# Two leading weight pieces of a fused attention and SwiGLU kernel: each load cut into two transfers over unequal numbers of partitions

## Chip, cores and metric

The kernel runs on one core of a Trainium2 chip. The metric is the device time of one execution in microseconds (us). The core has five engines that run side by side, each in its own program order: TensorE (PE in the profile, its weight loads as PEld), VectorE (DVE), ScalarE (ACT), GpSimd (POOL) and SyncE (SP), which here issues nearly all the transfers. Transfers are carried out by 16 DMA engines. An engine waits for another, or for a transfer, through semaphores.

## The reference

Lightning attention with a decay for each head feeds a SwiGLU layer. Cut to what is computed (4 batches, 8 heads, 768 positions, 64 wide; 3072 tokens, model width 512, hidden width 1536):

```python
for b in range(nb):                                  # blocks of 64 positions
    intra = np.einsum('bhic,bhjc->bhij', qb, kb) * Dmask[None]
    intra = np.einsum('bhij,bhjd->bhid', intra, vb)
    inter = np.einsum('bhid,bhde->bhie', qb * lam_pow[None], kv_state)
    out[:, :, sl] = intra + inter
    kv_state = lam_block[None, :, None, None] * kv_state + \
        np.einsum('bhsd,bhse->bhde', kb * rev_pow[None], vb)
x = out.transpose(0, 2, 1, 3).reshape(3072, 512)
g = x @ w_gate                                       # 512 x 1536
y = (g / (1 + np.exp(-g)) * (x @ w_val)) @ w_out     # 1536 x 512
```

All inputs and the output are float32. The weights that matter here are `w_gate` and `w_val`.

## The kernel before

**Tiling.** Attention is done in 12 groups of 256 positions of one batch. Each pair of groups makes one token tile of 512 tokens, and the SwiGLU layer runs over six such tiles. A weight matrix of 512 x 1536 lies in SBUF as 128 partitions by 4 row chunks by 1536 columns in bfloat16 (`wg_sb`, `wv_sb`). The hidden width is walked in 12 columns blocks of 128, called `fc` below.

**Order.** The schedule is written out by hand: every engine executes its instructions in the order in which the code emits them. The stretch that the change touches is the start. SP (and for two transfers ACT) loads k, q and v of groups 0 and 1 in halves (line 100, `load_fp32`), and then the weights. The weights come as float32 pieces through `w_piece` (line 218 issues): a piece covers some columns of `w_gate` and the same columns of `w_val`, all 512 rows, as one transfer each. The first two pieces are one `fc` block wide (128 columns, 256 KB for each matrix); all later ones are two blocks wide (512 KB for each matrix). The raw float32 tiles come from a pool of ten buffers that k and q of later groups share; a narrow piece holds gate and value in one buffer.

After landing, a piece is cast to bfloat16. The first narrow piece is cast by GpSimd in lines 652 and 653, the second by GpSimd through `w_cast` (line 226), the gate part of a wide piece by ScalarE and its value part by GpSimd (line 226; the first value part in two halves at line 672). TensorE then uses it: line 519 is the gate product (`ffn_gate`), line 534 the value product (`ffn_val`). Block 0 is computed for half the tokens before group 1's attention is finished, and from block 2 on the blocks run over 512 tokens, with later transfers (`w_piece`, `load_group`) and casts attached to them as a plan. The load of group 2 (k, q) stands on SP after the weight pieces of blocks 6 to 9; its q is cast by GpSimd (line 278, `cast_half`) and transposed by TensorE (line 294, `pe_transpose`) after block 8. The output product is line 552.

In the raw load each partition receives 4 runs (one for each row chunk) of 128 columns, 512 bytes each, so one partition's share of a narrow transfer is 2 KB. All the loads in question stand in one queue:

```python
    w_piece(0, 1)
    w_piece(1, 2)
    w_piece(2, 4)
    w_piece(4, 6)
```

Of the kernel before, what the change touches and what calls it, by code (L numbers as in the profile page):

```python
# [19 lines left out]
@with_exitstack  # L20
def kernel(
    ctx: ExitStack,
    tc: tile.TileContext,
    q: bass.AP,
    k: bass.AP,
    v: bass.AP,
    lam: bass.AP,
    moe_w_gate: bass.AP,
    moe_w_val: bass.AP,
    moe_w_out: bass.AP,  # L30
    out: bass.AP,
):
    nc = tc.nc
    with tc.manual_schedule():
        _body(ctx, tc, nc, q, k, v, lam, moe_w_gate, moe_w_val, moe_w_out, out)


def _body(ctx, tc, nc, q, k, v, lam, moe_w_gate, moe_w_val, moe_w_out, out):
# [169 lines left out]
    wv_d = moe_w_val.rearrange("(c p) f -> p c f", p=128)  # L208
    wo_d = moe_w_out.rearrange("(c p) m -> p c m", p=128)

    def w_piece(c0, c1, eng=None):
        cs = slice(c0 * 128, c1 * 128)
        n = (c1 - c0) * 128
        if n == 128:
            both = raw_pool.tile([128, 2, MC, n], FP32, name="wraw", tag="raw")
        for j, (w_sb, w_d) in enumerate(((wg_sb, wg_d), (wv_sb, wv_d))):
            t = both[:, j] if n == 128 else raw_pool.tile([128, MC, n], FP32, name="wraw", tag="raw")
            (eng or nc.sync).dma_start(out=t, in_=w_d[:, :, cs])  # L218
            w_raw.append((w_sb[:, :, cs], t))

    w_raw = []
# [364 lines left out]
    new_xt(0)  # L586
    new_xt(1)
    POOLC = nc.gpsimd.tensor_copy
    w_piece(0, 1)
    w_piece(1, 2)  # L590
    w_piece(2, 4)
    w_piece(4, 6)
    cast_half(0, 0, (None, DVEC))
# [234 lines left out]
```

## Time and profile before

| | |
|---|---|
| median of four executions | 228.18 us (227.41 to 228.92) |
| profiled execution | 227.41 us, of which the traced span is 225.70 us |
| PE busy | 218.9 us, 97% of the span |
| VectorE, ScalarE, GpSimd busy | 91.6, 106.4, 89.3 us |
| granted TensorE clock, mean | 0.999 |
| read from HBM, written to HBM | 28.31 MB, 6.29 MB |
| transfers of narrow weight pieces (gate, value) | 2 and 2 of 256 KB, median 5.8 us from issue to landing |
| transfers of wide weight pieces (gate, value) | 5 and 5 of 512 KB, 7.0 and 6.5 us |
| first k, q and v transfers | 256 KB each, landing after 3.4 to 4.7 us |

Times in the profile are counted from the start of the span. A row of the timeline gives the start, the duration from first to last of the merged instructions, the engine, the line, the operation and the tiles (written <- read), the count, and in brackets how long the engine was idle before it and what ended that. "SPq" stands for SP's issuing of a transfer; its duration is the time in which SP was occupied by the issue, not that of the data. The chain of waits is the path that ended last, followed back from the last instruction.

### The profile page before, as it was taken

The numbers are of one execution on the slowest core, as the hardware profiler recorded it, in microseconds if no ns is written. First come the engines' busy times: TensorE is split into PE (matmuls) and PEld (weight loads), VectorE is DVE, ScalarE is ACT, GpSimd is POOL, SyncE is SP. The second block draws the span as 40 slices with busy tenths as digits, with TensorE's granted clock in tenths as the row PEclk, the third lists the DMA queues.
The fourth block names the chain that finished last, engine by engine and source line by source line (L and its number), as shares of the span: only waits on it lengthen the run. The fifth ranks groups of instructions, "written<-read, shape, count | busy, mean of one in ns | idle before, by whom it ended". The sixth has DMA issues, their size and how long they took to land.

```text
span 225.7 us, 6028 instructions
## 1 busy us (share of the span) xinstructions
PE 218.9 (97%) x2492; PEld 122.3 (54%) x2504; DVE 91.6 (41%) x157; ACT 106.4 (47%) x211; POOL 89.3 (40%) x133
## 2 busy tenths in 40 slices
PE   8889999999999999999999999999999999999994
PEld 4666445888886456454544544544544444444442
DVE  2764357585853711734335262253242123222200
ACT  5878575755563253564553553553533423322321
POOL 6675737727791122869553171191150000000000
PEclk9999999999999999999999999999999999999999
DMA  6999999999997998396787849907101101101122
GB/s 197 342 337 339 371 362 325 217 175 331 405 256 165 247 259 211 85 231 157 187 192 199 217 98 231 232 7 139 49 1 46 49 0 46 46 3 46 46 93 93
DMA packets 88028, 39.70 MB, mean 176 GB/s; under 512 B 57666, under 2 KB 83522, under 8 KB 88002
## 3 DMA queue, kind: packets, MB, share of 16 engines
q1 hardware_dynamic: 83490, 32.58, 55.9%
q10 hardware_dynamic: 4512, 6.75, 8.4%
q8 instruction: 19, 0.31, 0.5%
q14 instruction: 7, 0.06, 0.1%
HBM read 28.31 MB, written 6.29 MB: 153 GB/s over the span
## 4 chain that ended last, share of the span: by engine, by line
PE 84%; DMA 7%; SPq 6%; issue 1%; POOL 0%; ACT 0%; DVE 0%; DVEq 0%
PE bank L552 27%; PE bank L519 25%; PE bank L534 24%; DMA qraw<-in_q_dram 4%; DMA wraw<-in_moe_w_val_dram 3%; SPq L100 3%; SPq L218 3%; PE bank L479 2%; PE bank L466 2%; PE bank L387 1%; PE bank L331 1%; PE bank L357 1%; PE bank L294 1%; POOL qk L278 0%; SPq L114 0%
## 5 line engine op out<-in xcount | busy, mean ns | idle before, releaser
L537 DVE TENSOR_TENSOR h<-sil,bank 128x512 bf16<-128x512 bf16 (+1 forms) x91 | 51.9, 576 | 104.0 <-PE bank L534 86.6
L519 PE MATMUL bank<-xt,wg_sb 128*128 128x512 bf16 (+1 forms) x364 | 77.2, 335 | 0.0
L534 PE MATMUL bank<-xt,wv_sb 128*128 128x512 bf16 (+1 forms) x364 | 77.1, 335 | 0.0
L523 ACT ACTIVATE sil<-bank 128x512 bf16<-128x512 f32 (+1 forms) x91 | 46.3, 513 | 43.0 <-PE bank L519 38.4
L552 PE MATMUL bank<-wo_sb,h 128*128 128x512 bf16 (+2 forms) x288 | 64.2, 370 | 0.7 <-issue 0.2
L534 PEld LDWEIGHTS <-wv_sb 128*128 128x128 bf16 x364 | 35.4, 98 | 26.9 <-POOL wv_sb L226 0.3
L519 PEld LDWEIGHTS <-wg_sb 128*128 128x128 bf16 x364 | 34.1, 98 | 26.0 <-DVE xt L491 0.3
L552 PEld LDWEIGHTS <-h 128*128 128x128 bf16 x300 | 28.7, 98 | 32.7
L554 ACT COPY osb<-bank 128x512 f32<-128x512 f32 (+1 forms) x24 | 14.0, 582 | 55.7 <-PE bank L552 53.0
L243 POOL TENSOR_TENSOR v_s<-v,dec 128x1024 bf16<-128x1024 f32 (+1 forms) x15 | 24.4, 1635 | 33.4 <-DMA v<-in_v_dram 33.1
L426 POOL TENSOR_TENSOR kvf<-kvs,ups 128x256 f32<-128x256 f32 x8 | 5.8, 727 | 29.7 <-ACT ups L409 27.1
L338 DVE TENSOR_TENSOR ssb<-bank,causal 128x512 bf16<-128x512 f32 x24 | 15.3, 684 | 4.7 <-PE bank L331 4.7
L491 ACT CAST xt<-bank 128x512 bf16<-128x512 f32 x19 | 11.6, 656 | 3.2 <-PE bank L479 2.7
L435 POOL CAST kvn<-kvf 64x256 bf16<-64x256 f32 x24 | 11.4, 476 | 1.5
L426 POOL TENSOR_TENSOR kvf<-kvf,ups 128x256 f32<-128x256 f32 x16 | 11.6, 726 | 0.6
L409 ACT COPY ups<-bank 128x256 f32<-128x256 f32 (+1 forms) x24 | 9.5, 450 | 1.5 <-PE bank L387 1.0
L263 ACT CAST qk<-kraw 128x1024 bf16<-128x1024 f32 x9 | 9.4, 1041 | 1.3 <-DMA kraw<-in_k_dram 0.8
L265 DVE TENSOR_TENSOR qk<-qraw,qdn 128x1024 bf16<-128x1024 f32 x6 | 8.2, 1368 | 2.6 <-DMA qraw<-in_q_dram 2.6
L362 DVE TENSOR_TENSOR ssb<-bank,causaln 128x512 bf16<-128x512 f32 x12 | 8.3, 688 | 1.4 <-PE bank L357 1.2
L479 PE MATMUL bank<-ssb,v_s 64*64 64x128 bf16 (+1 forms) x384 | 6.8, 208 | 0.5 <-ACT guard L450 0.5
L479 PEld LDWEIGHTS <-v_s 64*64 64x64 bf16 x384 | 5.6, 105 | 1.8 <-issue 1.1
L387 PE MATMUL bank<-v_s,qk 64*64 64x64 bf16 x352 | 5.8, 195 | 0.5 <-issue 0.5
(66 smaller groups left out, 122.6 us busy)
## 6 DMA issues: line engine op xcount, KB each, us to landing
out_dram<-osb ACTq DMA_DIRECT2D x23, 256.0 KB, 2.7
v<-in_v_dram SPq DMA_DIRECT2D x18, 256.0 KB, 4.7
woraw<-in_moe_w_out_dram SPq DMA_DIRECT2D x6, 512.0 KB, 7.6
kraw<-in_k_dram SPq DMA_DIRECT2D x24, 128.0 KB, 3.4
qraw<-in_q_dram SPq DMA_DIRECT2D x24, 128.0 KB, 3.6
wraw<-in_moe_w_gate_dram SPq DMA_DIRECT2D x5, 512.0 KB, 7.0
wraw<-in_moe_w_val_dram SPq DMA_DIRECT2D x5, 512.0 KB, 6.5
kraw<-in_k_dram SPq DMA_DIRECT2D x4, 512.0 KB, 6.4
```

What stands on the lines that cost most here:

```text
L243: eng.tensor_tensor(out=st[("vs", g)][:, h0:h1], in0=st[("v", g)][:, h0:h1].rearrange("p h (s d) -> p h s d", s=2), in1=vfac(g, h0, h1), o ...
L338: nc.vector.tensor_tensor(out=ssb[:, h2, 2 * c:2 * c + 2].rearrange("p a s n -> p a (s n)"), in0=sp[(c, h2)].rearrange("p (a x) -> p a x", ...
L426: nc.gpsimd.tensor_tensor(out=o, in0=f, in1=u, op=ALU.add)
L435: nc.gpsimd.tensor_copy(out=o[64 - h2 * 64:128 - h2 * 64], in_=f[h2 * 64:h2 * 64 + 64])
L479: nc.tensor.matmul(op[r][h2 * 64:h2 * 64 + 64, cols(g, hp, s)], v_s[ps, 2 * hp + h2, s], ssb[ps, h2, hp * 2 + s] if g >= NAT0 else ssb[ps, ...
L491: fns[r](out=xt[:, g % 2, :, r].rearrange("p h (m s) -> p h s m", s=2) if g < NAT0 else xt[:, g % 2, :, :, r * M:r * M + M], in_=op[r].rea ...
L519: nc.tensor.matmul(gp[:, 0:N], wg_sb[:, mc, fs], xt[:, b0 // 2:b1 // 2, mc].rearrange("p g b n -> p g (b n)"), start=(mc == 0), stop=(mc = ...
L523: nc.scalar.activation(sil[:, 0:N], gp[:, 0:N], AF.Silu)
L534: nc.tensor.matmul(vp[:, 0:N], wv_sb[:, mc, fs], xt[:, b0 // 2:b1 // 2, mc].rearrange("p g b n -> p g (b n)"), start=(mc == 0), stop=(mc = ...
L537: nc.vector.tensor_tensor(out=h_sb[:, fc % FH, b0:b1].rearrange("p b n -> p (b n)"), in0=sil[:, 0:N], in1=vp[:, 0:N], op=ALU.mult)
L552: nc.tensor.matmul(ps, st[("h", t, fc // FH)][:, fc % FH, b], wo_sb[:, fc, c0:c1], start=(fc == 0), stop=(fc == FC - 1))
L554: fn(out=osb[:, c0:c1], in_=ps)
```

## The change

`w_piece` gets a list of partition ranges for the gate and for the value transfer, and issues one transfer for each range. By default there is one range of all 128 partitions. For the first two pieces the ranges are unequal: 120 and 8 partitions for both transfers of piece 0, 88 and 40 for the gate and 104 and 24 for the value transfer of piece 1. So four transfers become eight, on the same queue at the same place, with the same bytes to the same tiles. The casts still read whole tiles.

```diff
-    def w_piece(c0, c1, eng=None):
+    def w_piece(c0, c1, eng=None, cuts=(((0, 128),),) * 2):
         cs = slice(c0 * 128, c1 * 128)
         n = (c1 - c0) * 128
         if n == 128:
             both = raw_pool.tile([128, 2, MC, n], FP32, name="wraw", tag="raw")
         for j, (w_sb, w_d) in enumerate(((wg_sb, wg_d), (wv_sb, wv_d))):
             t = both[:, j] if n == 128 else raw_pool.tile([128, MC, n], FP32, name="wraw", tag="raw")
-            (eng or nc.sync).dma_start(out=t, in_=w_d[:, :, cs])
+            for p0, p1 in cuts[j]:
+                (eng or nc.sync).dma_start(out=t[p0:p1], in_=w_d[p0:p1, :, cs])
             w_raw.append((w_sb[:, :, cs], t))
...
-    w_piece(0, 1)
-    w_piece(1, 2)
+    w_piece(0, 1, cuts=(((0, 120), (120, 128)),) * 2)
+    w_piece(1, 2, cuts=(((0, 88), (88, 128)), ((0, 104), (104, 128))))
     w_piece(2, 4)
     w_piece(4, 6)
```

## The prediction, made before the changed kernel was run

> **What bounds the kernel now.** I read the page's busy table first, then the chain of waits in order of time for the first 34 us, then the timeline by engine around the weight pieces. The page's head and the chain:
>
> ```profile
> span 225.7 us, 6028 instructions
> ...
> PE 218.9 (97%) x2492; PEld 122.3 (54%) x2504; DVE 91.6 (41%) x157; ACT 106.4 (47%) x211; POOL 89.3 (40%) x133
> ...
> PE 84%; DMA 7%; SPq 6%; issue 1%; POOL 0%; ACT 0%; DVE 0%; DVEq 0%
> ```
>
> TensorE is the bound over the whole span; transfers and their issue hold 13% of the chain. The chain by time shows where:
>
> ```profile
> 11.60 2.10 SPq L218
> ...
> 15.14 7.37 DMA wraw<-in_moe_w_val_dram
> ...
> 22.56 0.20 POOL wv_sb L226
> 22.76 8.24 DMA qraw<-in_q_dram
> 31.00 0.05 issue
> 31.05 0.63 POOL qk L278
> 31.68 0.04 issue
> 31.73 1.18 PE bank L294 x16
> ```
>
> Up to 31.73 us the chain is SP's load stream; from there to the end it is TensorE. So what the change does must be read at 31.73 and at whatever holds TensorE before that. TensorE's rows there, and the casts that feed it:
>
> ```profile
> 14.53 0.61 POOL L652 CAST wg_sb<-wraw 128x512 bf16<-128x512 f32 x1 [0.90 <-DMA wraw<-in_moe_w_gate_dram]
> 15.25 0.62 POOL L653 CAST wv_sb<-wraw 128x512 bf16<-128x512 f32 x1
> 15.98 0.62 POOL L226 CAST wg_sb<-wraw 128x512 bf16<-128x512 f32 x1
> 16.77 0.62 POOL L226 CAST wv_sb<-wraw 128x512 bf16<-128x512 f32 x1 [0.17 <-DMA wraw<-in_moe_w_val_dram]
> 19.42 1.18 POOL L672 CAST wv_sb<-wraw 128x512 bf16<-128x512 f32 x2 [2.04 <-DMA wraw<-in_moe_w_val_dram]
> ```
>
> ```profile
> 14.82 0.48 PEld L479 LDWEIGHTS <-v_s 64*64 64x64 bf16 x32 [0.21 <-issue]
> 15.39 0.33 PEld L519 LDWEIGHTS <-wg_sb 128*128 128x128 bf16 x4
> ...
> 20.09 0.66 PEld L534 LDWEIGHTS <-wv_sb 128*128 128x128 bf16 x4 [0.21 <-POOL wv_sb L672]
> ...
> 23.66 0.55 PEld L534 LDWEIGHTS <-wv_sb 128*128 128x128 bf16 x4 [0.32 <-POOL wv_sb L226]
> ...
> 31.72 0.34 PEld L294 LDWEIGHTS <-qk 128*128 128x128 bf16 x6 [0.61 <-POOL qk L278]
> ```
>
> GpSimd waits 0.90 us for the first gate piece, but TensorE does not: the cast ends at 15.14 and TensorE is busy with line 479 until 15.39. Between 14.15 and 31.60 its matmuls have no gap over 60 ns; the idle weight loads (0.21, 0.32 us) lie beside running matmuls. At 31.60 it stops for 0.13 us, for q of group 2. **So in this stretch the transfers and TensorE are tied: the casts for 20.09, 23.66 and 31.73 arrive just in time.** Transfers that land earlier win about 0.2 us (the last matmul before 31.73 holds the array 0.50 us against 0.21 us of a steady one, and some 0.1 us of that is the usual drain before a narrow product, as at 34.25 us); transfers that land later are paid in full.
>
> **What the change removes, adds and moves.**
>
> *The late completion.* The trace has sixteen completion marks for a transfer, one for each DMA engine. For the first gate piece fifteen come between 12.44 and 13.04, the last at 14.47; the three narrow transfers behind it show the same (last marks at 15.20, 15.93 and 16.71, each about 1.4 us after the other fifteen). The v transfer ahead of it has all sixteen within 0.78 us. So one DMA engine fell 1.4 us behind at about 12 us, where the trace has a 16 KB instruction fetch of 0.94 us (11.96 to 12.89). It stays behind: the marks of q of group 2 run from 29.45 to 30.39, and one at 31.00, the one that the chain follows.
>
> *How the load shifts.* The Trainium skill ("DMA: Bandwidth & Descriptors", section "Why a DMA increments its semaphore by 16 and not by 1") says that a transfer runs on the largest k up to 16 that divides its outermost sizes, for SP's queue the lowest-numbered k engines. No run so far shows a k between 1 and 16. By it 120 partitions go to 15 engines, 8 to 8, 88 to 11, 40 to 10, 104 to 13 and 24 to 12. Rows (2 KB each) over the four transfers, 32 for each engine before: engines 0 to 7: 9+9+12+10 = 40; 8 and 9: 38; 10: 34; 11: 26; 12: 24; 13 and 14: 16; 15: 0. The sum is 512 as before.
>
> *What a row costs.* The four narrow issues start at 8.65, 9.38, 10.12 and 10.86, and their fifteen early marks follow in the same step: 0.74 us for 8 rows of an engine, 0.092 us a row, 354 GB/s in all. The packets take a constant 27 ns each, which speaks for a pace set by each engine and not shared: I take it that idle engines make the busy ones no faster. Then engines 0 to 7 end 8 x 0.092 = 0.74 us later, 8 and 9 0.55, 10 0.18, while 11 gains 0.55, 12 0.74, 13 and 14 1.48, 15 up to 2.96. If the pace were shared after all, the overload would cost nothing. I take 0.74 and keep 0.
>
> *Rule and row.* The same page's "Rules for kernel authors" advises against two transfers over disjoint partition parts: they share the engines, so one 128-partition transfer is to be used. By that rule alone this is pure loss: four issues more. The row says that one engine's lateness, 1.4 us, is more than the worst overload, 0.74 us. By the rule the sum is 0 to +0.74 us, by the row -0.2 (all that TensorE can take) if the late engine is among 11 to 15. I go by the row, since the rule counts engines that are equally far.
>
> *Which engine is late?* The marks carry no number. The skill's section "Latency and other measured facts" says that engines 7 and 15 are usually slower than the rest; in this trace two engines do come last in the transfers before (0.58 and 0.60 us after the first, the others by 0.44). 15 would be relieved wholly, 7 loaded with 0.74 more. This is the main unknown.
>
> *Four issues more on SP.* The trace has issues of 128 rows unhindered at 0.42 to 0.51 us (first k and v loads) and the one-row `lam` at 0.34, plus 0.04 between. A long part at 0.5 and a short one at 0.36 make 0.94 a pair instead of 0.74, SP comes to the first wide piece at 12.4 instead of 11.60. Its issue occupies SP for 2.10 us, to 13.69, with the queue full: the 0.8 us are hidden there. One more wait: eight completion semaphores are used in turn, and an issue waits for the eighth one before it. With eight parts in the line the first wide piece waits for the first part (about 13.1 us), and so it would be out by about 13.7 to 13.9, as now. The engines have work until about 15.3, so they don't run dry. Behind SP's wait stand only the later loads. Cost nothing; without that cover, up to 0.8 us.
>
> *The casts.* A cast of a narrow piece waits for two semaphores instead of one; at most 0.1 us on GpSimd, which has 0.9 us of idle time to give there.
>
> **The sum,** against the profiled execution (227.41; its span 225.70). Late engine among 11 to 15: the first gate piece lands at 13.04 + 0.09 = 13.13, before GpSimd is free (13.62); its cast ends at 14.3 instead of 15.14, and TensorE gains nothing, being busy until 15.39. Second piece: 14.51 + 0.55 = 15.06 and 15.32 + 0.74 = 16.06, instead of 15.93 and 16.71. From then on engines 0 to 9 decide. At 22.51 (value of blocks 4 and 5) the others' last mark is 21.96; plus 0.74 is at most 22.70. At 31.00 (q) it is 30.39, so 30.4 to 31.13. TensorE: -0.2 to +0.2; I take -0.1: 227.3. The profiled execution is 0.77 below the median, so in the median's terms **228.1 us.**
>
> **Rivals.**
>
> 1. *Late engine among the loaded ones (0 to 10).* Every mark that decides comes 0.18 to 0.74 later. Second piece's casts: 0.55 - 0.05 and 0.74 - 0.11 of delay for TensorE; at 20.09, 23.66 and 31.73 0.74 with no slack. Not additive, one delay: +0.2 to +0.75, 228.4 to 228.9. For it: eleven of the sixteen engines. Against: the skill's 15.
> 2. *Slower: SP can't issue the parts in time.* Mechanism: uneven parts take longer to issue, or wait for the eighth issue before. SP reaches the first wide piece at 8.65 + 8x; its data begin about 1.2 us after the issue begins (the first q: issue 0.81, packets from 2.0), so the engines run dry from x = 0.68 on (14.1 us). At x = 1.0 they stand still about 2.5 us, the values at 20.09 and 22.51 come that much later, TensorE waits: +2.2, 230.4. It decides from x of about 0.85. For it: no row has such a part. Against: issues are 0.34 to 0.51 where the queue has room.
> 3. *Faster by over 0.5%.* The median is 0.77 above the profiled execution; were all of that late transfers, and the change removed it and the 0.3 us here, 227.1. Against: TensorE has 2.1 us of gaps in the whole span, most before 14.2 us, where no weight is used.
> 4. *The parts are spread over all engines after all.* Nothing changes but the issues: 228.2.
>
> **How the numbers follow.** Likeliest case 0.38, rival 1 0.25, rival 2 0.19, rival 3 0.12, rival 4 0.06. A measurement of this kernel can tell about 0.5% (1.14 us) from no change. Faster: 0.12 and 0.01 of the first. Slower: 0.19 and 0.04 of rival 1's tail. The rest, 0.64, is no change. Range 227.1 (rival 3) to 229.7 (all of rival 1, and rival 2 up to x = 0.9); rival 2 beyond is left out. The likeliest case's own range is 227.8 to 228.5.
>
> **What would show it.** Right: GpSimd's 0.90 us before line 652 gone and that cast at about 13.65; the wait at 23.66 and the start of line 294 at 31.73 within 0.2 us of now; eight SP rows of 0.35 to 0.7 us; the first wide piece issued by about 13.9. Rival 1: L652 at 14.6, L294 at 32.4. Rival 2: SP rows of 0.9 us and more, a long wait before 19.35 to 20.09. Wrong altogether: a difference that arises after 32 us.

## The result, and the profile after

The changed kernel is slower: 228.96 us (228.00 to 231.17, median of 37 executions) against 227.91 us (226.91 to 229.50, 58 executions) of the kernel before. The ratio is 1.0047 with a 95% interval of 1.0034 to 1.0061, a loss of 1.07 us (0.8 to 1.4). That is a little inside the half per cent that the prediction called no change, and inside its range, but it is clear of noise, and the likeliest case had expected 0.1 us in the other direction.

The profiled execution took 228.47 us with a span of 226.7. Its page, where the first was 225.7 and 84% TensorE on the chain:

```profile
span 226.7 us, 6036 instructions
...
PE 77%; DMA 13%; SPq 4%; POOL 4%; issue 1%; ACT 0%; DVE 0%; DVEq 0%; POOLq 0%
```

The share of transfers on the chain has doubled. Its pieces in order of time (start, duration, what) from the first weights on; lines are one higher than before:

```profile
9.81 6.44 DMA wraw<-in_moe_w_val_dram
16.24 0.02 issue
16.26 0.37 SPq L219
16.63 0.04 issue
16.67 6.96 DMA wraw<-in_moe_w_val_dram
23.64 0.05 issue
23.69 0.33 POOL wv_sb L227
24.02 8.17 DMA qraw<-in_q_dram
32.19 0.05 issue
32.24 0.63 POOL qk L279
32.87 0.05 issue
32.91 1.18 PE bank L295 x16
```

The transposes of q of group 2 start at 32.91 instead of 31.73: q landed 1.19 us later. On the way there, SP did not issue a wide piece until 16.26, when a value transfer issued at 9.81 had landed. GpSimd's casts and TensorE's weight loads, from the timelines of the two engines:

```profile
13.55 0.61 POOL L653 CAST wg_sb<-wraw 128x512 bf16<-128x512 f32 x1
16.36 0.62 POOL L654 CAST wv_sb<-wraw 128x512 bf16<-128x512 f32 x1 [2.20 <-DMA wraw<-in_moe_w_val_dram]
...
23.69 1.04 POOL L227 CAST wv_sb<-wraw 128x1024 bf16<-128x1024 f32 x1 [0.89 <-DMA wraw<-in_moe_w_val_dram]
```

```profile
15.23 0.30 PEld L388 LDWEIGHTS <-qk 64*64 64x64 bf16 x27 [1.33 <-issue]
...
24.78 0.55 PEld L535 LDWEIGHTS <-wv_sb 128*128 128x128 bf16 x4 [0.37 <-POOL wv_sb L227]
...
32.91 0.67 PEld L295 LDWEIGHTS <-qk 128*128 128x128 bf16 x10 [0.67 <-POOL qk L279]
```

The first gate cast is where the prediction put it (13.55; its wait is gone). But three things stand here that were not there before, and each could be the 1.07 us: SP's pause to 16.26; a longer stop of TensorE inside line 388, for which the profile shows no releaser (1.33 us in this row of weight loads, 0.64 before; 1.24 us and 0.55 us in the rows of the matmuls, as which the stop is given from here on); and q landing later. TensorE's wait for q is hardly longer (0.67 us, 0.61 before), as the stop had made TensorE itself 1.1 us late by then.

The trace also settles how the parts were spread. A part of 120 partitions has 15 completion marks, 8 has 8, 88 has 11, 40 has 10, 104 has 13 and 24 has 12, as the rule in the Trainium skill has it that the prediction draws on ("DMA: Bandwidth & Descriptors", "Why a DMA increments its semaphore by 16 and not by 1"). And they place the late engine. The 120-row value part has one mark at 16.24, fourteen by 14.25; the 8-row part behind it (engines 0 to 7), the 88- and 40-row parts (0 to 10) have no late mark; and the two early marks of the 104-row part (15.15 and 15.28) are those of engines 11 and 12, which had no part of the gate transfer before it. So the late one is 13 or 14. It is among those that the change relieves (16 rows instead of 32, all 16 in the 120-row parts), and still the kernel is slower.

A fourth view, by which most of the experiments can be read, is the table of busy times by stretch: the last column is what the transfers moved, in GB/s, the one before it the mean busy share of the 16 DMA engines (over 1 where packets of one engine overlap). Before, and then after:

```profile
13.00:14.00 1.00, 0.60 (x21) 0.30 (x13) 1.00 (x3) 1.00 (x3) 0.63 (x1) 1.00 1.15 336
14.00:15.00 1.00, 0.85 (x42) 0.60 (x45) 0.63 (x2) 0.67 (x2) 0.47 (x1) 1.00 1.13 298
15.00:16.00 1.00, 1.00 (x38) 0.68 (x32) 0.50 (x1) 0.16 (x1) 0.77 (x3) 1.00 1.02 318
16.00:17.00 1.00, 1.00 (x16) 0.82 (x16) 0.25 (x2) 0.96 (x2) 0.83 (x2) 1.00 1.11 384
```

```profile
13.00:14.00 1.00, 0.79 (x21) 0.54 (x22) 1.00 (x3) 1.00 (x4) 0.91 (x2) 1.00 1.05 240
14.00:15.00 1.00, 0.00 (x0) 0.00 (x0) 1.00 (x2) 0.69 (x2) 0.17 (x1) 1.00 1.11 221
15.00:16.00 1.00, 0.78 (x38) 0.52 (x41) 0.02 (x1) 0.32 (x1) 0.00 (x0) 1.00 1.20 218
16.00:17.00 1.00, 1.00 (x36) 0.68 (x34) 0.42 (x1) 0.21 (x2) 0.64 (x2) 1.00 1.13 255
```

In these 4 us the kernel before moves 1336 KB, the changed one 934: 402 KB less, which at the 368 GB/s of the later stretch (20 to 32 us) is 1.1 us of transfer time.

### The profile page after: what moved, and what is told of

Same layout as the page of the kernel before. It is cut to its first block, busy times and chain, and to the rows that moved or that the text cites. A ratio compares the mean times of both kernels' runs of the same rounds, so it can differ in the third digit from the quotient of the medians.

```text
span 226.7 us, 6036 instructions
## 1 busy us (share of the span) xinstructions
PE 219.4 (97%) x2492; PEld 122.6 (54%) x2504; DVE 91.3 (40%) x157; ACT 106.6 (47%) x211; POOL 90.7 (40%) x133
## 4 chain that ended last, share of the span: by engine, by line
PE 77%; DMA 13%; SPq 4%; POOL 4%; issue 1%; ACT 0%; DVE 0%; DVEq 0%; POOLq 0%
PE bank L553 26%; PE bank L520 22%; PE bank L535 22%; DMA wraw<-in_moe_w_val_dram 6%; DMA qraw<-in_q_dram 4%; SPq L100 3%; DMA v<-in_v_dram 3%; POOL v_s L244 2%; PE bank L480 2%; PE bank L467 2%; PE bank L388 1%; PE bank L358 1%; DMA out_dram<-osb 1%; POOL qk L266 1%; PE bank L332 1%
## 5 line engine op out<-in xcount | busy, mean ns | idle before, releaser
L520 PEld LDWEIGHTS <-wg_sb 128*128 128x128 bf16 x364 | 34.1, 98 | 26.0 <-DVE xt L492 0.3
L244 POOL TENSOR_TENSOR v_s<-v,dec 128x1024 bf16<-128x1024 f32 (+1 forms) x15 | 24.9, 1667 | 31.5 <-DMA v<-in_v_dram 31.2
L436 POOL CAST kvn<-kvf 64x256 bf16<-64x256 f32 x24 | 12.5, 520 | 1.5
```

Source lines behind the costliest of these rows:

```text
L244: eng.tensor_tensor(out=st[("vs", g)][:, h0:h1], in0=st[("v", g)][:, h0:h1].rearrange("p h (s d) -> p h s d", s=2), in1=vfac(g, h0, h1), o ...
L436: nc.gpsimd.tensor_copy(out=o[64 - h2 * 64:128 - h2 * 64], in_=f[h2 * 64:h2 * 64 + 64])
L520: nc.tensor.matmul(gp[:, 0:N], wg_sb[:, mc, fs], xt[:, b0 // 2:b1 // 2, mc].rearrange("p g b n -> p g (b n)"), start=(mc == 0), stop=(mc = ...
```

## The experiments

The theories: *wait* (SP waits for the eighth transfer before, and with more transfers in the line it meets one with a late mark), *fetch* (TensorE's stop for instructions grew), *overload* (engines 0 to 10 carry more rows), and, formed on the way, *transfer cost* (each transfer costs each of its engines something besides its rows).

**One piece cut at a time.** Only piece 0, then only piece 1:

```diff
     w_piece(0, 1, cuts=(((0, 120), (120, 128)),) * 2)
-    w_piece(1, 2, cuts=(((0, 88), (88, 128)), ((0, 104), (104, 128))))
+    w_piece(1, 2)
```

> Piece 0 cut as in the change (120 and 8, both transfers), piece 1 whole: six narrow transfers instead of eight. Three theories for the 1.0 us. Wait theory (SP's issue of the first block-4/5 gate piece waits for the eighth transfer before it, the 120-row value transfer with its late mark): here the transfer eight before is the first gate part, done by about 13.3 us, so SP loses at most 0.3 us at that place and the kernel is within 0.3 us of before. Fetch theory (TensorE's stop inside line 388 for want of instructions grew from 0.55 to 1.24 us): the stop stays as long as in the changed kernel, if the late engine still has its full share in piece 0, and the kernel is slower by about 0.7 us. Overload theory (engines 0 to 7 carry 8 rows more): here 2 rows more, 0.18 us, so slower by 0.2 us at most.

Measured: 227.56 us, ratio 1.0001 (0.9981 to 1.0021). The stop inside line 388 was 0.28 us, q landed at 31.06.

```diff
-    w_piece(0, 1, cuts=(((0, 120), (120, 128)),) * 2)
+    w_piece(0, 1)
     w_piece(1, 2, cuts=(((0, 88), (88, 128)), ((0, 104), (104, 128))))
```

> Piece 0 whole, piece 1 cut as in the change (88 and 40, 104 and 24). Wait theory: the transfers eight before the wide pieces are the whole transfers of piece 0, whose late marks come at about 14.5 and 15.2 us, when SP has got to blocks 4/5 anyway: slower by at most 0.3 us. Fetch theory: nothing changes before the fetch at about 12 us, so the stop is as before (0.55 us) and the kernel no slower. Overload theory: engines 0 to 7 carry 6 rows more, 0.55 us, and the kernel is slower by 0.4 to 0.6 us.

Measured: 228.19 us, ratio 1.0025 (1.0004 to 1.0047), as the overload theory had it; no stop at all. But q landed early here, at 30.45, and TensorE's lateness arose after 59 us in the profile. So piece 0's cuts cost nothing alone, piece 1's about half of the loss, and the two together perhaps more than the sum: the intervals are too wide to say.

**Equal halves: the same number of transfers, no imbalance.**

```diff
-    w_piece(0, 1, cuts=(((0, 120), (120, 128)),) * 2)
-    w_piece(1, 2, cuts=(((0, 88), (88, 128)), ((0, 104), (104, 128))))
+    w_piece(0, 1, cuts=(((0, 64), (64, 128)),) * 2)
+    w_piece(1, 2, cuts=(((0, 64), (64, 128)),) * 2)
```

> All four narrow transfers cut in equal halves of 64 partitions: eight transfers as in the change, but every engine carries what it carried before. Wait theory: the same stall or more, since every half has the late engine in it: SP waits about 2 us before the block-4/5 gate piece and the kernel is slower by 0.7 to 1.3 us. Overload theory: no loss. Fetch theory: the stop is as before or a little longer, 0 to 0.7 us.

Measured: 229.78 us, ratio 1.0066 (1.0039 to 1.0093). That is at least the loss of the change itself (the intervals overlap), so eight transfers cost time with no engine carrying a row more. But the stall that the wait theory had expected is not there: SP issues the eight halves one after another, about 0.65 us each, and comes to the first wide piece at 14.30 us instead of 11.60. A half is 128 KB, and 128 KB in 0.65 us is 202 GB/s: in this kernel SP's issue is slower than the engines, which is the prediction's second rival at 0.70 us a transfer. In the stretch of 13 to 17 us the engines' busy share is 0.82 and 195 GB/s are moved. The first five halves, for which the engines still have a queue, have their median marks at 12.64, 13.11, 13.58, 14.02 and 14.41: about 0.45 us for 4 rows of each engine, more than half of the 0.74 us for 8.

**Relieving engines 13 to 15 from the start.**

```diff
-    w_piece(0, 1, cuts=(((0, 120), (120, 128)),) * 2)
-    w_piece(1, 2, cuts=(((0, 88), (88, 128)), ((0, 104), (104, 128))))
+    w_piece(0, 1, cuts=(((0, 104), (104, 128)),) * 2)
+    w_piece(1, 2)
```

> Piece 0 cut into 104 and 24 for both transfers (13 and 12 engines), piece 1 whole. In the changed kernel the marks place the late engine at number 13 or 14, of which the 120-row parts make full use. Here engines 13 to 15 carry nothing of piece 0, engines 0 to 11 two rows more a transfer. If the late engine is 13 or 14: the marks of piece 0 have no straggler, GpSimd's wait for the first gate piece is gone, and TensorE's stop, if the fetch shares that engine's queue, is shorter than 0.55 us: faster than before by 0.2 to 0.6 us. If the stop doesn't depend on that engine's load: same as before. Overload theory: 4 rows more, slower by up to 0.37 us.

Measured: 227.76 us, ratio 0.9999 (0.9971 to 1.0027). The marks of piece 0 have no straggler, as hoped (all within 0.7 us), and yet nothing is gained: TensorE's stop is 0.54 us as before, and q lands at 31.24. This agrees with the profile before, where the first gate cast ended at 15.14 and TensorE took it up at 15.39: a straggler of the first gate piece was not on the path there. (A gain hidden by the cost of the two added transfers is not ruled out by this run alone.)

**Taking away SP's pause.** In the change SP's long pause is for the 120-row value part. Cut at 104 that part leaves the late engine out:

```diff
-    w_piece(0, 1, cuts=(((0, 120), (120, 128)),) * 2)
+    w_piece(0, 1, cuts=(((0, 120), (120, 128)), ((0, 104), (104, 128))))
     w_piece(1, 2, cuts=(((0, 88), (88, 128)), ((0, 104), (104, 128))))
```

> The changed kernel with one cut moved: the value transfer of piece 0 in 104 and 24 instead of 120 and 8, so that the late engine (13 or 14 by the marks) has no part of it; eight transfers and eight issues as before the edit, engines 0 to 11 one row more. Wait theory: the transfer that SP waits for before the block-4/5 gate piece has no late mark and is done by about 14.5 us, SP's stall of 2.0 us and GpSimd's 2.2 us before the first value cast go, and the kernel is 0.5 to 1.0 us faster than the changed one, within 0.2% of the kernel before. Overload theory: nothing is gained, 1.0047 or a little more. Issue theory (eight issues of 0.3 to 0.6 us make SP late by themselves): nothing is gained either.

Measured: 228.74 us, ratio 1.0043 (1.0028 to 1.0059): nothing gained. SP's rows around the place, in the changed kernel and then here:

```profile
13.31 0.39 SPq L219 DMA_DIRECT2D wraw<-in_moe_w_gate_dram  x1
13.74 0.51 SPq L219 DMA_DIRECT2D wraw<-in_moe_w_val_dram  x1
16.26 0.37 SPq L219 DMA_DIRECT2D wraw<-in_moe_w_gate_dram  x1
```

```profile
14.51 0.39 SPq L219 DMA_DIRECT2D wraw<-in_moe_w_gate_dram  x1
14.95 0.50 SPq L219 DMA_DIRECT2D wraw<-in_moe_w_val_dram  x1
15.49 1.56 SPq L219 DMA_DIRECT2D wraw<-in_moe_w_gate_dram  x1
```

The pause of 2.0 us before the third of these rows is gone, and q lands at 32.59, no earlier than in the change. But the expectation's premise did not hold: in this kernel the late engine was another, 8 or 9 by its marks, so the first wide piece waited for the 120-row gate part, from 13.86 to 14.51. The pause was moved and shortened, not taken away. That SP's waits cost nothing is not shown by this run.

**Overload alone.** The kernel before with one transfer added; its data are not used:

```diff
     w_piece(1, 2)
+    nc.sync.dma_start(out=wo_sb.bitcast(FP32)[0:8].rearrange("p c (a n) -> p (c a) n", n=128),
+                      in_=bass.AP(tensor=moe_w_out.tensor, offset=moe_w_out.offset,
+                                  ap=[[24 * DM, 8], [DM, 24], [1, 128]]))
     w_piece(2, 4)
```

> The kernel before with one extra transfer behind piece 1: 8 partitions of 24 runs of 512 bytes from w_out into a part of wo_sb that is overwritten later (its data are not used), so engines 0 to 7 get 6 rows more and nothing is cut; one issue more. Overload theory: the marks of engines 0 to 7 come 0.55 us later from then on, slower by 0.3 to 0.55 us (1.0013 to 1.0024). Wait and issue theories: no loss, within 0.1 us (1.0000 to 1.0005).

Measured: 228.16 us, ratio 1.0022 (1.0004 to 1.0040), inside what the overload theory expected. The size is not clean: its eight marks came about 1.7 us after those of the transfer ahead, not 0.55, so these scattered rows cost more than rows of a weight piece. Load on engines 0 to 7 costs time, then, but this run does not give its price.

**The changed kernel and the kernel before, again.**

> The changed kernel again, for a second profile. Wait theory: SP's long pause before the block-4/5 gate issue (to 16.26 us in the first profile) is there again, and so is a late mark of the 120-row value transfer. Fetch theory: TensorE's stop inside line 388 is again above 1 us. If the stop is 0.3 to 0.6 us here, its 1.24 us were a matter of the one execution.

> The kernel before again, for a second profile: how far two executions of one program differ in TensorE's start (0.39 us between the two profiles at 9 us, where no weight transfer has been issued), in the stop inside line 387 (0.55 us) and after 59 us. Fetch theory: the stop is again near 0.5 us. If these places differ by several tenths here too, differences of that size between profiles are not the change's.

> The changed kernel for a third profile. Transfer-cost theory: most marks of the first wide gate piece at 17.9 to 18.3 us (16.4 to 16.8 before), most marks of q of group 2 at 30.7 us or later, its last mark at 31.8 us or later, whatever SP's pauses; TensorE late by at least 0.8 us at line 295 and stop inside line 388 not above 0.6 us in most executions. Fetch theory: the stop is above 1 us.

Single executions of 231.06 us (change), 229.45 (before) and 228.21 (change). The stop inside line 388 (387 before) was 0.45, 0.47 and 0.33 us: the 1.24 us of the first profile belonged to that execution, and the fetch theory falls. So does the 0.39 us by which TensorE was late at 9 us in that profile. What recurs is the transfers: q landed at 34.47 and 32.18 in the change, at 31.19 in the kernel before. TensorE's weight loads in the third profile of the change:

```profile
14.15 0.32 PEld L388 LDWEIGHTS <-qk 64*64 64x64 bf16 x27 [0.42 <-issue]
...
20.21 0.55 PEld L520 LDWEIGHTS <-wg_sb 128*128 128x128 bf16 x4 [0.68 <-ACT wg_sb L227]
21.09 0.55 PEld L535 LDWEIGHTS <-wv_sb 128*128 128x128 bf16 x4 [0.34 <-POOL wv_sb L673]
...
32.90 0.17 PEld L295 LDWEIGHTS <-qk 128*128 128x128 bf16 x3 [0.90 <-POOL qk L279]
```

TensorE is on time at 14.15 (14.15 in the kernel before), loses 0.9 us by 20.21 to waits for weights and is 1.2 us late at q. And SP's pause is in another place: it issues the first wide piece at 14.69 instead of 13.31, the next two without a pause. Most marks of that piece come at 17.9 to 18.3 us all the same, 18.2 to 18.4 with the early issue, 16.4 to 16.8 in both profiles of the kernel before. So an issue 1.4 us earlier does not bring the data earlier. That the wait is free does not follow: with the late issue the engines were partly idle between 16 and 17 us, with a busy share of 0.72 here and 0.78 in the second profile against 1.13 in the first. In the first profile they were busy, but slowly so (255 GB/s). The rows of the second and the third profile:

```profile
16.00:17.00 1.00, 0.69 (x13) 0.49 (x12) 0.24 (x1) 0.96 (x2) 1.00 (x2) 1.00 0.78 229
16.00:17.00 1.00, 0.90 (x13) 0.51 (x12) 0.26 (x1) 0.94 (x2) 0.96 (x2) 1.00 0.72 214
```

The wait may be a part of the loss in two of the three profiles; the runs do not separate it.

**SP's side alone.** The kernel before with four one-row transfers, whose data are not used:

```diff
     w_piece(1, 2)
+    for n in range(4):
+        nc.sync.dma_start(out=pad[0:1, n * H:n * H + H],
+                          in_=bass.AP(tensor=lam.tensor, offset=lam.offset, ap=[[0, 1], [1, H]]))
     w_piece(2, 4)
```

> The kernel before with four one-row transfers of lam (32 bytes each, into a scratch tile that nothing reads) behind piece 1. SP gets four issues more and the wait for the eighth transfer before moves by four, as in the change: the first wide gate piece must wait for the late mark of the first narrow transfer (about 14.4 us), the next ones for those of the other three (about 15, 15.8 and 16.6 us). The engines' load is unchanged, except for engine 0 (four descriptors). Wait theory (and issue theory): slower by 0.7 to 1.3 us, as much as the change or more, with q of group 2 landing at 32 us or later. Transfer-cost theory, formed from the marks of the eight-part kernels (each transfer costs each of its engines about 0.18 us beside 0.07 us a row, so that eight parts cost engines 0 to 7 some 1.3 us): SP's pauses are covered by the queue, q of group 2 lands within 0.3 us of before and the kernel is within 0.15% of it.

Measured: 228.44 us, ratio 1.0032 (1.0016 to 1.0048): more than I had expected from the transfer-cost theory, at the low end of what the wait theory expected. The stretches:

```profile
13.00:14.00 1.00, 0.80 (x25) 0.39 (x14) 1.00 (x3) 1.00 (x3) 0.18 (x1) 1.00 1.06 312
14.00:15.00 1.00, 0.08 (x9) 0.07 (x12) 0.60 (x2) 0.27 (x1) 1.00 (x2) 1.00 0.77 225
15.00:16.00 1.00, 1.00 (x38) 0.55 (x40) 0.00 (x0) 0.37 (x1) 0.98 (x3) 0.63 0.52 80
16.00:17.00 1.00, 1.00 (x34) 0.77 (x27) 0.11 (x1) 0.08 (x1) 0.84 (x2) 0.50 0.94 292
```

The first wide piece waits for the late mark of the first narrow one (14.40) and is issued at 14.42; by then the engines, with no load added, have run dry: busy share 0.52 and 80 GB/s. That this is what the kernel pays for is not shown: q landed at 31.74, 0.6 to 0.7 us later than before, but in this execution TensorE never waited for it, being late already. It had stood 1.07 us for v of group 1 (to 14.92) and then had half the clock, both of which began with a transfer issued before the added ones. The four marks also give a price: 15.38, 15.59, 15.80 and 16.02, so a transfer takes about 0.21 us of its engine here though it moves 32 bytes.

**Fewer transfers.** Pieces 0 and 1 loaded as one, cast in halves:

```diff
-    w_piece(0, 1)
-    w_piece(1, 2)
+    w_piece(0, 2)
...
-    POOLC(out=wg0, in_=wg0r)
-    POOLC(out=wv0, in_=wv0r)
+    POOLC(out=wg0[:, :, 0:128], in_=wg0r[:, :, 0:128])
+    POOLC(out=wv0[:, :, 0:128], in_=wv0r[:, :, 0:128])
...
-    w_cast((POOLC, POOLC))
+    POOLC(out=wg0[:, :, 128:256], in_=wg0r[:, :, 128:256])
+    POOLC(out=wv0[:, :, 128:256], in_=wv0r[:, :, 128:256])
```

> The other direction: pieces 0 and 1 as one piece of 256 columns, two transfers instead of four, same bytes, the casts each on its half. Transfer-cost theory: two transfers less on every engine, so the wide pieces and q of group 2 land 0.1 to 0.4 us earlier; the first gate cast begins up to 0.2 us later, still before TensorE needs it. TensorE can take about 0.2 us: 0 to 0.2% faster, or the same. Wait theory: SP has two issues less, no wait falls away that held it: the same.

Measured: 227.72 us, ratio 0.9998 (0.9977 to 1.0019). The cast of q and TensorE's use of it:

```profile
30.06 1.17 POOL L278 CAST qk<-qraw 128x512 bf16<-128x512 f32 x2 [2.00 <-DMA qraw<-in_q_dram]
```

```profile
31.57 0.48 PEld L294 LDWEIGHTS <-qk 128*128 128x128 bf16 x5
```

q is cast 1.0 us earlier than before, and TensorE loads it 0.15 us earlier and with no wait; its transposes begin at 31.78, as before (31.73). Landing earlier wins nothing; only landing later is paid.

**Piece 1 alone, again.**

> The kernel with only piece 1 cut again, for a second profile, since its first one had q of group 2 landed early (30.45 us) while its runs were 0.25% slower. Transfer-cost theory: engines 0 to 7 carry two transfers and 6 rows more (0.8 us by 0.21 us a transfer and 0.066 us a row); where the second instruction fetch falls on one of them, q lands after 31.3 us here and TensorE starts line 295 later than 31.8. If q lands early again and the loss is elsewhere, the loss of this kernel is not explained by the load.

Measured: one execution of 228.33 us beside 228.39 of the kernel before. q landed at 31.70, TensorE's line 295 started at 32.42 with no wait: TensorE was late already, having stood 0.29 us at 15.75 and 0.56 us at 21.37 for casts of weights. In this profile the load explains the lateness, by the weights and not by q. In the other, TensorE was on time at q (31.66, before 31.73) and the loss arose after 59 us; where that comes from stays open.

**The kernels side by side.** Rate is what the transfers moved between 13 and 17 us. "Worked out" is the deficit against the kernel before (339 GB/s, mean of its two profiles) over 4 us, divided by 368 GB/s, less the 0.2 us that TensorE can absorb:

| kernel | rate, GB/s | worked out, us | measured ratio | in us |
|---|---|---|---|---|
| before | 334, 344 | | 1 | |
| one merged piece | 385 | 0 | 0.9998 | 0.0 |
| piece 0 only | 314 | 0.1 | 1.0001 | 0.0 |
| 104 and 24, piece 0 | 314 | 0.1 | 0.9999 | 0.0 |
| piece 1 only | 279, 272 | 0.5 | 1.0025 | 0.6 |
| the change | 233, 218, 222 | 1.0 | 1.0047 | 1.1 |
| value part cut at 104 | 238 | 0.9 | 1.0043 | 1.0 |
| four one-row transfers | 228 | 1.0 | 1.0032 | 0.7 |
| equal halves | 195 | 1.4 | 1.0066 | 1.5 |

(For the change: (339 - 224) x 4 / 368 - 0.2 = 1.05.) The kernel with the extra transfer is left out, as its 279 GB/s hold data that nobody uses. The sizes rest on one to three profiles a kernel, the 4 us were chosen after the fact, and the ratios have intervals of about 0.3 to 0.6 us to each side, but the order is the same in both columns except for the one-row transfers. **The loss goes with the rate of the load stream in those 4 us.** What lowers the rate is a sum whose parts the runs do not separate: the transfers' own cost, fewer engines at work on a part, slower packets (below) and, in some executions, SP's wait.

## Why the prediction was wrong, step by step

**The tie of transfers and TensorE: right.** The loss arises at the weights of the first blocks and at q of group 2, and nothing after that is needed to explain it: from the first transpose of q to the end of the span it is 194.0 and 194.2 us in the two profiles before, and 193.8, 194.2 and 193.6 in the three of the change. That TensorE could win only about 0.2 us was right too: a stream 1.0 us earlier won nothing.

**How the load shifts, and which engine is late: right.** The parts ran on 15, 8, 11, 10, 13 and 12 engines, and in all three profiles of the change the engine that fell behind furthest at 12 us was 13 or 14, the likeliest case's premise (in the third, one of engines 0 to 7 was late as well, by about 0.7 us). Its conclusion did not follow. For the first piece it could not: the sum has that piece land at 13.13 with a late engine anywhere from 11 to 15, but the 120-row parts leave engines 11 to 14 their full 8 rows each. The value part had its last mark at 16.24, 15.86 and 15.67 (15.20 before). The passage of the Trainium skill that was cited for engine 15 ("DMA: Bandwidth & Descriptors", "Latency and other measured facts") was weak evidence here: it calls its guess at the cause specific to transfers whose descriptors GpSimd writes, and these were SP's.

**The step that failed is the price of the load: "0.092 us a row", and so 0.74 us for engines 0 to 7.** I took the 0.74 us of a whole 8-row transfer as 8 rows. It holds a part for the transfer itself, an estimated 0.21 us if the one-row transfers stand for it, which leaves 0.53, or 0.066 a row. (The halves agree: 0.21 + 4 x 0.066 is 0.47, measured 0.45.) Eight transfers with 40 rows are then 8 x 0.21 + 40 x 0.066 = 4.32 us on each of engines 0 to 7, against 4 x 0.74 = 2.96 before: 1.36 us more, not 0.74. The median marks of the first wide gate piece came 1.3 to 1.7 us later than before. Seen as a rate, piece 1 runs mostly on ten engines, and 10/16 of the 354 GB/s of a full transfer are 221; the stretch shows 218 to 255.

**With it failed "the packets take a constant 27 ns", from which I took the pace to be each engine's own.** Between 11 and 18.5 us, 1% of the 512-byte packets took longer than 28 ns in the first profile of the kernel before. In the three profiles of the change it is 51, 44 and 42%, with a mean of 34.1, 31.9 and 31.7 ns against 27.2. So from the median mark of the v transfer ahead to that of the last narrow part it took 5.1, 4.7 and 4.5 us in the change and 3.0 in both profiles before, 1.5 to 2.1 us more, and more than the estimate of 1.36. What slows the packets stays open. The kernel with only piece 0 cut has it too (48%) and loses nothing.

**"The row says 1.4 us of lateness is more than the overload": the wrong comparison.** It set the worst engine before against the worst engine after, as if the late one were a fixed amount. But instruction fetches go on: in the first profile of the change one runs from 19.15 us for 0.9 us, and the next wide gate piece has one mark at 22.34, 1.3 us behind the other fifteen (by 21.06). At q two marks are behind, 32.09 and 32.19; the other fourteen come by 30.95. The prediction misread the same place before: it took q's marks to end at 30.39 but for one at 31.00, where the trace has two, 30.95 and 31.00. So with the late engine relieved another would still have landed q at 30.95, and its 30.4 was never to be had. In the kernel before, the stragglers fell behind engines that were on time. In the change they fall behind a pack that is late already: q's median mark came at 30.8, 31.4 and 30.7 against 30.2 and 29.4, its last at 32.2, 34.5 and 32.2 against 31.0 and 31.2. Here the skill's rule against two transfers over halves of the partitions (in "Rules for kernel authors") was the better guide, and for more than the sharing of engines that it names: it promises no gain, and equal halves lost 1.5 us.

**Rival 1** had the mechanism, rows on the low engines, and was mis-sized by the same term; its condition, that the late engine be one of the loaded, was not needed. **Rival 2** was right about equal halves (0.70 us an issue, engines partly idle), not about the change: its eight issues took 0.3 to 0.72 us and the first wide piece was out at 13.7 to 15.1. The wait for the eighth transfer, which I had costed at nothing, is real (SP stood still for 1.2 to 2.0 us, at a place that differs between executions). What it cost in the change stays open, as said above.

**Four issues more, the casts:** hidden in the first profile only. GpSimd waited 2.20 us for the value part there, but TensorE's line 535 was not held by it (17.35, with no idle time shown before it). In the second and third profiles its weight loads waited 0.47 and 0.26 us at this place for the cast of that part.

## What to carry to other kernels

Before cutting a transfer to steer load away from a slow DMA engine, price the transfer itself and not only its rows, and work out the rate of the whole set while the parts run: engines left out are bandwidth left out, and on a stream that is just in time that can be paid in full. A straggler is worth removing only if an engine waits for it on the path; look first at whether the cast behind it has slack. When two profiles of the same program are at hand, discard every difference that they show between themselves: here that took away one of the three suspects and put another in doubt.

## What the runs showed of the hardware that was not expected

*A pause of TensorE can be followed by half the clock.* In the second profile of the kernel before, v of group 1 had its late mark at 13.62 us, and TensorE waited inside line 387:

```profile
13.91 0.22 PE L387 MATMUL bank<-v_s,qk 64*64 64x64 bf16 x4 [0.47 <-issue]
14.79 0.38 PE L387 MATMUL bank<-v_s,qk 64*64 64x64 bf16 x24 [0.66 <-POOL v_s L243]
```

The stretches after it (the third column from the right is the granted clock):

```profile
12.00:15.50 3.50, 2.13 (x65) 1.40 (x67) 2.46 (x6) 2.43 (x6) 2.28 (x4) 1.00 1.11 327
15.50:19.00 3.50, 3.50 (x50) 2.31 (x51) 0.73 (x1) 1.36 (x4) 1.58 (x3) 0.51 1.04 348
```

The clock was granted at half for 3.41 us (15.58 to 18.99), and TensorE went from 0.9 us behind the first profile (line 519 at 16.33, there 15.39) to 2.1 us (line 534 at 19.71, there 17.60); this execution took 229.45 us, the first 227.41. The same happened in the profiles with the extra transfer and with the one-row transfers, each after a stop for v (0.83 and 1.07 us). A pause alone does not do it: in the first profile of the change TensorE was busy for 2.02 of the 3.5 us from 12 to 15.5, here for 2.13, and there the clock stayed full. What else it takes stays open. The half clock is a part of why executions of one program spread over 2.6 us, and not the change's loss: the mean clock was under 0.995 in 6 of the change's 38 executions, and the other 32 have a median of 228.92 us.

*The late engine is not always the same.* It was 13 or 14 in the change (three profiles) and 8 or 9 in the kernel with the value part cut at 104. In every profile a 16 KB instruction fetch of 0.9 to 1.2 us, beginning at 11.2 to 12.5 us, goes ahead of it. That the fetch is what holds the engine is likely from this order, not shown. A cut that is made for one engine can't follow it.
